# A two-layer decode step in fp32: a ring of 24 KB in place of 28, four KB of K kept across the layers, and one weight tile laid on 20 rows in place of 16

## The chip, the core and the metric

The kernel runs on one core of a Trainium2 chip. The core has a matrix engine (TensorE, in the profile PE for matmuls and PEld for its weight loads), three engines for elementwise work (VectorE or DVE, ScalarE or ACT, GpSimd or POOL), a queue engine that here issues nearly all transfers (SyncE or SP), and sixteen DMA engines that move data between HBM and the on-chip memory of 128 partitions (rows). The metric is the device time of one execution in microseconds.

## The reference

Two layers, each an attention block and a gated feed-forward block, for one new token of four sequences, all in fp32. The same weights and the same caches serve both layers.

```python
B, Sq, D = 4, 1, 512        # Hq, Hkv, Sk, Dh = 32, 8, 4096, 128 ; F = 1792
# A: q = layernorm(x) @ wq ; p = softmax(q k^T / sqrt(Dh)) ; x + (p v) @ wo
# B: h = silu(n @ w1) * (n @ w3), n = layernorm(x) ; x + h @ w2
x = x + _A_ref(_layernorm(x, axis=-1), A_k_cache, A_v_cache, A_wq, A_wo)
x = x + _B_ref(_layernorm(x, axis=-1), B_w1, B_w3, B_w2)
x = x + _A_ref(_layernorm(x, axis=-1), A_k_cache, A_v_cache, A_wq, A_wo)
x = x + _B_ref(_layernorm(x, axis=-1), B_w1, B_w3, B_w2)
```

K and V hold 67 MB each and are needed once in each layer; the weights are 28 MB.

## The kernel before

**Memory.** Nearly all on-chip memory is one tile, `arena` (line 46), of 216 KB on each of 128 partitions. All addresses below are KB in a partition; one KB there is 128 KB of data. Three regions have fixed places: wq at 0 to 64 (WQ), wo at 64 to 128 (WO) and a kept V at 128 to 192 (KEPT). The transposed probabilities pT take the last 2 KB (PT, line 52). What is left in the first feed-forward, 192 to 216 and the first 4 KB of wo's region, is the ring: 28 KB.

**Loads.** `plan` (line 86) is a list of all loads in order: source, KB, keys, and an address or None. `pump` (line 165) issues loads on SP, in this order only, as long as `take` (line 56) finds the place free; `done` (line 196) and `vacate` return a place and call `pump` again. This happens while the program is written out, so the order of SP's instructions and of the places is fixed. On the chip each load then waits only for the instructions that last used its addresses, and for an earlier load's landing, since the loads share eight completion semaphores in turn.

**Layer 0** goes through the eight groups of K and V in order. K of a group is one load of 64 KB a row, and so is V. While K of one group is read, V of the group before is loaded, and so on in turn, in two places (64 and 128). V of the last group (`TURN` = 7) goes to KEPT and stays for layer 1, which takes the groups in the reverse order. wq and wo stay too.

**The ring** (lines 124 to 140). With wq, wo and the kept V in place, the first feed-forward's weights pass through the ring in pieces of one load each: w1 and w3 in two parts ("a" of four 4 KB pieces, "b" of four 3 KB pieces), w2 in seven 4 KB pieces. They are followed by K of the last group for layer 1: its first 32 KB as eight "half" pieces of 4 KB (half of a block of 512 keys), seven of them in the ring. The eighth and all later loads go where `take` finds room, at first in wq's place, whose tiles layer 1's query projection frees one after the other (`q_product`, line 333). TensorE reads the pieces in the order w1a, w3a, w1b, w3b 0 and 1, w2 0, w3b 2 and 3, w2 1 to 6 (`feed_forward`, lines 542 to 587); then come the normalisation and the query projection, and only then the half pieces (`scores`, line 384). The addresses of the pieces, given by `slots`, say which earlier piece a load must wait for: w2 i and half i lie at `slots[i]`; w3b 2 lies where w3a 1 and w3a 3 were; w2 5 waits for w3b 2.

**The tile on few rows.** In the last feed-forward, the first tile of w2 (128 rows of 512) is loaded as 16 rows of 16 KB, `w2s`, by four loads of every fourth row (lines 151 and 154; `pump` takes a slice of rows from line 169 on, line 177 issues it). Each is put ahead of one of w1a, w3a, w1b, w3b. Eight units of 16 rows are then multiplied (`few`, line 536, with `columns`, line 531), four before and four after w3b's product. The hidden values for them come from eight small matmuls (line 562) and one copy (line 567).

## Time and profile before

| | us |
|---|---|
| median of three runs | 706.02 (705.9 to 706.09) |
| the profiled execution | 705.91 |
| its span, first to last instruction | 704.1 |
| mean granted TensorE clock in it | 0.813 of full speed |

The page gives the busy time of each engine in the span, forty slices of the span with the busy share of each engine and of the sixteen DMA engines in tenths, the queues of the DMA engines, and groups of instructions by line. Further views answer for a stretch: busy time and DMA share by window, instructions in order of time with what they waited for, issues of loads with their time to landing. Times in them are from the span's start. In the first layer the groups of K and V last until 337 us; the ring stage is from about 345 to 400; the last feed-forward begins at about 682. A DMA share of 1 means that all sixteen engines have a packet under way; packets on one engine overlap slightly, so it can pass 1. The queue q1 is SP's loads; q8 loads instructions.

### The profile page before, as it was taken

How to read it: one execution, taken by the hardware profiler on the slowest of the kernel's cores; microseconds unless marked ns; L12 is line 12 of the kernel's file. 1: busy time of each engine (PE TensorE's matmuls, PEld its weight loads, DVE VectorE, ACT ScalarE, POOL GpSimd, SP SyncE). 2: the span in 40 equal slices, each digit the busy share in tenths (PEclk: the TensorE clock that was granted, in tenths of full speed). 3: DMA queues.
4: the chain of work that ended last, by engine and by line, in shares of the span. 5: the costliest groups of instructions: out<-in, count | busy, mean ns of one | idle time of the engine just before them, and what ended most of it. 6: DMA issues, size and time to landing. Idle time of an engine off the chain costs nothing. (4 is left out here: it accounts for less than half of the span.)

```text
span 704.1 us, 7082 instructions
## 1 busy us (share of the span) xinstructions
PE 408.4 (58%) x3174; PEld 136.0 (19%) x3174; DVE 85.1 (12%) x291; ACT 36.8 (5%) x85; POOL 2.9 (0%) x10
## 2 busy tenths in 40 slices
PE   2555453456556454547788894364553545477687
PEld 1112011112111111112243231021120111122134
DVE  2001010101001010101111111011000101010111
ACT  0000000000000000002001000000000000000100
POOL 0000000000000000000000000000000000000000
PEclk9986787767777776879999988679787868689899
DMA  9999999999999999999999999999999999999997
GB/s 417 432 403 473 418 417 422 462 418 432 451 421 422 436 448 421 440 408 435 410 405 403 410 437 440 439 436 422 432 455 417 433 432 440 421 433 420 426 425 298
DMA packets 13749, 299.37 MB, mean 425 GB/s; under 512 B 1671, under 2 KB 1799, under 8 KB 6407
## 3 DMA queue, kind: packets, MB, share of 16 engines
q1 hardware_dynamic: 13584, 298.92, 99.2%
q8 instruction: 25, 0.41, 0.2%
q14 instruction: 5, 0.04, 0.0%
q10 hardware_dynamic: 135, 0.01, 0.0%
HBM read 298.85 MB, written 0.07 MB: 425 GB/s over the span
## 5 line engine op out<-in xcount | busy, mean ns | idle before, releaser
L438 PE MATMUL o_ps<-arena 128*32 128x512 f32 x1024 | 148.6, 730 | 147.8 <-DMA arena<-in_v 133.0
L393 PE MATMUL s_ps<-arena,qpad 128*32 128x512 f32 x1024 | 146.2, 725 | 88.0 <-DMA arena<-in_kt 88.0
L438 PEld LDWEIGHTS o_ps<-arena 128*32 128x32 f32 x1024 | 37.7, 130 | 256.8 <-issue 224.5
L393 PEld LDWEIGHTS s_ps<-arena,qpad 128*32 128x32 f32 x1024 | 39.3, 130 | 178.1 <-issue 170.6
L447 DVE SCALAR_TENSOR_TENSOR p<-o_ps,parts,p 128x512 f32<-128x512 f32 x16 | 12.0, 751 | 272.7 <-PE o_ps L438 272.7
L400 DVE TENSOR_REDUCE top<-s_ps 128x1 f32<-128x512 f32 x16 | 11.1, 691 | 190.8 <-PE s_ps L393 190.8
L281 PE MATMUL m_ps<-ident,rows 128*32 128x256 f32 (+2 forms) x90 | 25.2, 376 | 0.0
L445 ACT ACTIVATE p<-o_ps,parts 128x512 f32<-128x512 f32 x16 | 11.0, 687 | 195.8 <-PE o_ps L438 186.9
L337 PE MATMUL o_ps<-arena,xpad 128*32 128x512 f32 x112 | 15.4, 675 | 7.8 <-DMA arena<-in_wq 7.8
L424 PE MATMUL t_ps<-ident,p 128*128 128x128 f32 x64 | 11.4, 305 | 13.5 <-ACT p L418 13.5
L451 PE MATMUL t_ps<-ident,p 128*128 128x128 f32 x64 | 10.5, 287 | 13.9 <-DVE p L447 13.8
L411 ACT ACTIVATE f<-d 128x1 f32<-128x1 f32 x16 | 3.2, 203 | 253.1 <-DVE d L409 253.1
L473 PE MATMUL x_ps<-arena,oT 128*4 128x512 f32 x104 | 12.8, 592 | 6.3 <-DVE oT L459 3.5
L418 ACT ACTIVATE p<-s_ps,top 128x512 f32<-128x512 f32 x16 | 10.9, 684 | 76.7 <-PE t_ps L451 76.7
L425 DVE COPY arena<-t_ps 128x512 f32<-128x512 f32 x16 | 11.1, 691 | 9.7 <-PE t_ps L424 9.7
L451 PEld LDWEIGHTS t_ps<-ident,p 128*128 128x128 f32 x64 | 6.7, 141 | 28.0 <-DVE p L447 28.0
L424 PEld LDWEIGHTS t_ps<-ident,p 128*128 128x128 f32 x64 | 7.3, 150 | 22.3 <-ACT p L418 19.2
L281 PEld LDWEIGHTS m_ps<-ident,rows 128*32 128x32 f32 x90 | 9.4, 110 | 10.4 <-issue 6.3
L506 PE MATMUL o_ps<-arena,xpad 128*32 128x192 f32 (+1 forms) x128 | 8.1, 360 | 1.3 <-DMA arena<-in_w 1.2
L506 PE MATMUL s_ps<-arena,xpad 128*32 128x192 f32 (+1 forms) x128 | 7.9, 359 | 1.6 <-DMA arena<-in_w 1.5
L337 PEld LDWEIGHTS o_ps<-arena,xpad 128*32 128x32 f32 x112 | 3.6, 122 | 17.2 <-DMA arena<-in_wq 8.7
L533 PE MATMUL x_ps<-arena,qT 128*4 128x128 f32 (+1 forms) x168 | 5.9, 271 | 1.1 <-DMA arena<-in_w 1.1
(100 smaller groups left out, 137.3 us busy)
## 6 DMA issues: line engine op xcount, KB each, us to landing
arena<-in_v SPq DMA_DIRECT2D x4, 4096.0 KB, 37.3
arena<-in_w SPq DMA_DIRECT2D x17, 512.0 KB, 9.3
arena<-in_kt SPq DMA_DIRECT2D x8, 1024.0 KB, 10.5
arena<-in_kt SPq DMA_DIRECT2D x2, 4096.0 KB, 16.9
arena<-in_wq SPq DMA_DIRECT2D x1, 7168.0 KB
arena<-in_v SPq DMA_DIRECT2D x3, 2048.0 KB, 36.9
arena<-in_wo SPq DMA_DIRECT2D x1, 4096.0 KB, 24.5
arena<-in_kt SPq DMA_DIRECT2D x8, 512.0 KB, 8.0
```

Of the source, the lines that this page charges most:

```text
L281: nc.tensor.matmul(m_ps[turn["m"] ^ 1][0:32, (4 - w) * P:], rows, ident.unsqueeze(1).broadcast_to([P, w, P]), start=True, stop=True)
L337: nc.tensor.matmul(ps[32 * k:32 * k + 32, :], xpad[:, k, lo:lo + 32], w[:, k, :], start=first, stop=last)
L393: nc.tensor.matmul(s_ps[32 * b:32 * b + 32, :], qpad[:, b, lo:lo + 32], k[:, j, :], start=(blk == 0), stop=(blk == NB - 1))
L400: nc.vector.tensor_reduce(top[:, 0:1], s_ps, axis=AX.X, op=ALU.max, negate=True)
L424: nc.tensor.transpose(t_ps[:, i, :], p[:, i * P:(i + 1) * P], ident)
L425: nc.vector.tensor_copy(pT.rearrange("p i r -> p (i r)"), t_ps.rearrange("p i r -> p (i r)"))
L438: nc.tensor.matmul(o_ps[32 * b:32 * b + 32, :], pT[:, i, 32 * b:32 * b + 32], w[:, b, :], start=(i == 0), stop=(i == NI - 1))
L445: nc.scalar.activation(p, o_ps, AF.Copy, scale=st["parts"][:, 0:1])
L447: nc.vector.scalar_tensor_tensor(p, o_ps, st["parts"][:, 1:2], p, op0=ALU.mult, op1=ALU.add)
L451: nc.tensor.transpose(t_ps[:, j, :], p[:, j * P:(j + 1) * P], ident)
L473: nc.tensor.matmul(x_ps[r:r + B, :], left(2 * i + n), w(n), start=first, stop=False)
L506: nc.tensor.matmul(ps[32 * j:32 * j + 32, lo:lo + n], x32[:, k, :], w[:, j * n:(j + 1) * n], start=(k == 0), stop=(k == KC - 1))
```

## The change

It has three parts.

1. K of the last group in layer 0 is loaded in two parts: 4 KB to a place of its own at 212 (`FIRST`) and 60 KB to 132 to 192. The 4 KB part is the first half piece of layer 1; it is not given back in layer 0 and is not loaded again. pT moves to 210.
2. The ring is 192 to 212 and wo's first 4 KB: 24 KB. The pieces get new addresses. w2 0 is now loaded ahead of w3b 0 and not after w3b 1. What each load waits for follows from the addresses: w2 1 for w1b 3, w2 2 for w3b 0, w2 3 for w3b 1, w2 4 for w2 0, w2 5 for w3b 3, w2 6 for w2 1, half 1 and 2 for w2 2, half 3 to 6 for w2 3 to 6. TensorE's order stays.
3. w2's first tile is laid on 20 rows of 12 KB (six units of 20) and 8 rows of 2 KB (one unit of 8), `w2t`: four loads of five rows and two of four rows. There are seven units, four before and three after w3b's product. The first two loads are put ahead of w1a, the last two ahead of w3b, behind the fourth of `w2s`.

```diff
-FEW = 16
+FEW = 20
...
-    PT = ARENA - 2
-    free = [(WO, PT - WO)]
+    FIRST, PT = ARENA - 4, ARENA - 6
+    free = [(WO, PT - WO), (FIRST, 4)]
...
     def cache(which, layer, g, parts, skip=0):
         src = (kt if which == "k" else v)[g]
+        if (which, layer, g) == ("k", 0, TURN):
+            weights("half", src[:, 0:4 * KB], 0, (4,), 4, FIRST)
+            weights("half", src[:, 4 * KB:], 0, (60,), 4, KEPT + 4, 1)
+            return
...
-    slots = [WO] + [RING + 4 * i for i in (5, 4, 3, 2, 1, 0)]
-    for i in range(4):
-        piece("w1a", i, (slots[6], slots[1], slots[2], slots[3])[i])
-    for i in range(4):
-        piece("w3a", i, (slots[4], slots[5], slots[0], slots[6])[i])
-    for i in range(4):
-        piece("w1b", i, RING + 21 - 3 * i)
-    for i in range(2):
-        piece("w3b", i, RING + 9 - 3 * i)
-    piece("w2", 0, slots[0])
-    for i in range(2, 4):
-        piece("w3b", i, RING + 9 - 3 * i)
-    for i in range(1, 7):
-        piece("w2", i, slots[i])
-    for i in range(7):
-        piece("half", i, slots[i])
+    for name, places in (("w1a", (0, 16, 12, 8)), ("w3a", (4, None, 0, 16)), ("w1b", (13, 10, 7, 4)), ("w2", (None,)),
+                         ("w3b", (1, 16, 13, 10)), ("w2", (6, 2, 16, None, 12, 8)), ("half", (4, 0, 16, None, 12, 8))):
+        first = int(name == "half" or len(places) == 6)
+        for i, at in enumerate(places):
+            piece(name, first + i, WO if at is None else RING + at)
...
-    side = iter([(w2s[i::4], slice(i, FEW, 4)) for i in range(4)])
+    side = iter([(w2s[i::4], slice(i, FEW, 4), 0) for i in range(4)] + [(w2t[i::2], slice(i, 8, 2), 12) for i in range(2)])
...
         for name, w in (("w1", w1), ("w3", w3)):
             aside()
+            if name + part in ("w1a", "w3b"):
+                aside()
...
-                    a = take(n)
+                    a = take(14)
...
-            split = layer == 1 and g == TURN and blk < SPLIT
-            keys = [("half", layer, 2 * blk + i) for i in range(2)] if split else [("k", layer, g, blk)]
+            split = g == TURN and (layer == 0 or blk < SPLIT)
+            keys = [("half", layer if blk or i else 0, 2 * blk + i) for i in range(2)] if split else [("k", layer, g, blk)]
...
             for key in keys:
-                done(*key)
+                if layer or key[2] or not split:
+                    done(*key)
...
-                columns(slice(0, FEW), WT + u, arena[:, at:at + 2 * KB])
+                columns(slice(0, FEW if u < 6 else 8), WT + u, arena[:, at:at + 2 * KB])
...
-            for u in range(8):
-                nc.tensor.matmul(t_ps[0:FEW, 2, B * u:B * u + B], h[0:32, FEW * u:FEW * u + FEW], ident[0:32, 0:B],
+            for u in range(7):
+                n = FEW if u < 6 else 8
+                nc.tensor.matmul(t_ps[0:n, 2, B * u:B * u + B], h[0:32, FEW * u:FEW * u + n], ident[0:32, 0:B],
...
-        few(4, 8)
+        few(4, 7)
...
-        "w2s": lay(w2j[0, :P].reshape(8, FEW, D).transpose(1, 0, 2)).reshape(FEW, 8 * D),
+        "w2s": lay(w2j[0, :6 * FEW].reshape(6, FEW, D).transpose(1, 0, 2)).reshape(FEW, 6 * D),
+        "w2t": lay(w2j[0, 6 * FEW:P]),
```

More of the change, by code (lines that the diff above doesn't have):

```diff
@@ L38, in tile_decode_layers @@
 @with_exitstack
-def tile_decode_layers(ctx: ExitStack, tc: tile.TileContext, x, kt, v, wq, wo, w1, w3, w2, w2s, out):
+def tile_decode_layers(ctx: ExitStack, tc: tile.TileContext, x, kt, v, wq, wo, w1, w3, w2, w2s, w2t, out):
     nc = tc.nc
@@ L148, in tile_decode_layers @@
     cache("v", 1, 0, (32, 16, 16))
-    side = iter([(w2s[i::4], slice(i, FEW, 4)) for i in range(4)])
+    side = iter([(w2s[i::4], slice(i, FEW, 4), 0) for i in range(4)] + [(w2t[i::2], slice(i, 8, 2), 12) for i in range(2)])
     def aside():
-        plan.append((*next(side), "few", None))
+        src, rows, at = next(side)
+        plan.append((src, rows, "few", at))
     for part, per, at in (("a", 4, 0), ("b", 3, 16)):
@@ L175, in pump @@
                     where[keys] = a
-                a = where[keys]
+                a = where[keys] + at
                 nc.sync.dma_start(arena[per, a * KB:(a + n) * KB], src)
@@ L249, in tile_decode_layers @@
     oT = const.tile([P, HKV, REP, B], F32, name="oT")
-    hT = qT.rearrange("p h c -> p (h c)")[:, 0:(WT + 8) * B].rearrange("p (m b) -> p m b", b=B)
+    hT = qT.rearrange("p h c -> p (h c)")[:, 0:(WT + 7) * B].rearrange("p (m b) -> p m b", b=B)
     top = const.tile([P, 32], F32, name="top")
@@ L262, in tile_decode_layers @@
     p = const.tile([P, 512], F32, name="p")
-    pT = arena[:, PT * KB:ARENA * KB].rearrange("p (i r) -> p i r", i=NI)
+    pT = arena[:, PT * KB:FIRST * KB].rearrange("p (i r) -> p i r", i=NI)
     def small(name, n=1, bufs=1):
@@ L566, in feed_forward @@
         if not keep:
-            nc.vector.tensor_copy(hT[0:FEW, WT:WT + 8, :], t_ps[0:FEW, 2, 0:8 * B].rearrange("p (u b) -> p u b", b=B))
+            nc.vector.tensor_copy(hT[0:FEW, WT:WT + 7, :], t_ps[0:FEW, 2, 0:7 * B].rearrange("p (u b) -> p u b", b=B))
             gate(FA, FB)
@@ L624, in tile_decode_layers @@
             if layer and n == 0:
-                assert take(ARENA - PT, PT) == PT
+                assert take(FIRST - PT, PT) == PT
             if n + 1 < HKV:
@@ L632, in tile_decode_layers @@
         if layer == 0:
-            give(PT, ARENA - PT)
+            give(PT, FIRST - PT)
             pump()
```

## The prediction

> **What bounds the kernel now.** I read the page's engine, slice and packet lines first, then the long waits, then the transfers.
>
> ```profile
> PE 408.4 (58%) x3174; PEld 136.0 (19%) x3174; DVE 85.1 (12%) x291; ACT 36.8 (5%) x85; POOL 2.9 (0%) x10
> DMA  9999999999999999999999999999999999999997
> DMA packets 13749, 299.37 MB, mean 425 GB/s; under 512 B 1671, under 2 KB 1799, under 8 KB 6407
> q8 instruction: 25, 0.41, 0.2%
> DVE p L447 <- PE o_ps L438: 272.7, 16, 22.7
> PE o_ps L438 <- DMA arena<-in_v: 133.0, 14, 14.1
> PE s_ps L393 <- DMA arena<-in_kt: 88.0, 16, 12.2
> ```
>
> TensorE is busy 58% of the span and itself waits 133.0 + 88.0 us for V and K; the largest wait, VectorE's 272.7 us, only hangs behind it. The sixteen DMA engines are at 9 tenths or more in 39 of 40 slices. So the bound is bytes over rate, 299.37 MB at 425 GB/s = 704 us. A change is worth what it takes off the DMA engines, as long as none of them is left without queued work. The place to test is the stage with the small ring. The next view is the stage table: length, busy time of PE, PEld, DVE, ACT and POOL, granted clock, DMA share, GB/s.
>
> ```profile
> 345.00:400.00 55.00, 50.19 (x483) 20.37 (x483) 7.32 (x30) 4.08 (x10) 1.10 (x2) 1.00 1.02 404
> 400.00:640.00 240.00, 133.05 (x919) 39.26 (x922) 29.45 (x91) 10.77 (x27) 0.00 (x0) 0.78 1.00 433
> 380.00:382.00 2.00, 1.72 (x20) 0.66 (x20) 0.05 (x1) 0.00 (x0) 0.00 (x0) 1.00 0.96 381
> 388.00:390.00 2.00, 2.00 (x21) 1.14 (x17) 0.17 (x1) 0.00 (x0) 0.00 (x0) 1.00 1.07 385
> ```
>
> The share in the ring's 55 us is 1.02 (packets overlap a little, so just over 1 is full) and its rate is 404 against 433 GB/s: small pieces move more slowly, but nothing stands idle. The two weakest 2-us stretches still have 0.96 and 385 GB/s. The 28 KB ring covers its turn-round; how much is to spare must be worked out.
>
> **The change part by part.** *Four KB of K not loaded again.* The first half block of layer 1 stays from layer 0: one 512 KB transfer less. What such a piece takes shows where TensorE meets each piece as it lands:
>
> ```profile
> 360.07 0.64 PE L506 MATMUL s_ps<-arena,xpad 128*32 128x256 f32 x8 [0.23 <-DMA arena<-in_w]
> ...
> 365.21 0.16 PEld L506 LDWEIGHTS o_ps<-arena,xpad 128*32 128x32 f32 x8 [0.73 <-DMA arena<-in_w]
> ```
>
> Four pieces of 4 KB a row lie between these starts: 5.14 / 4 = **1.28 us** each, which comes off every engine's queue: -1.28. (At the page's mean rate it would be 0.524 MB / 425 GB/s = 1.23.) TensorE's matmuls are the same ones. Layer 0's last K now comes as 4 + 60 KB. The 4 KB piece has its own place and is issued a whole transfer earlier, with nothing waiting behind it on SP; it moves at the piece rate, 1.28 instead of 8.39 MB / 433 GB/s / 16 = 1.21: +0.07.
>
> The Trainium skill, "DMA: Bandwidth & Descriptors", section "Anatomy of one DMA", fits a transfer as about 2.0 us plus its bytes, which speaks against splitting loads and shortening the ring: where no queue covers the fixed part, each such load would pay it (rival 4). The pieces above follow each other at 1.28 us, so before the change a queue covers it.
>
> *Ring of 24 KB.* A slot is filled again only after TensorE has read it. I count, from the two orders in the diff, what is queued behind a piece when its slot's next load waits for it. Before, the least is 19 KB (w2 piece 5 waits for w3b piece 2; 3 + 16 KB lie between). After, it is 13 KB: w2 piece 2 waits for w3b piece 0, with three 3 KB pieces and one of 4 KB between; then 14 KB for w2 piece 3, and 16 KB or more otherwise. In time, by 0.32 us a KB: 6.1 us before, 4.2 us after. Against that stands the turn-round:
>
> ```profile
> 371.18 0.53 PE L506 MATMUL o_ps<-arena,xpad 128*32 128x192 f32 x8 [0.21 <-DMA arena<-in_w]
> 371.77 0.33 SPq L183 DMA_DIRECT2D arena<-in_w  x1
> arena<-in_wq SPq DMA_DIRECT2D x1, 1024.0 KB, 4.8
> ```
>
> 0.59 us from the matmul's start to SP's issue; then the way to the first byte, at most 4.8 - 2 x 1.28 = 2.2 us by the shortest landing of a 1 MB load. Together 2.8. So the slowest DMA engine keeps 4.2 - 2.8 = 1.4 us in hand (before 3.3).
>
> The second narrow place is the layer change, where the ring is full of K and the next space comes from wq:
>
> ```profile
> 382.72 0.33 SPq L183 DMA_DIRECT2D arena<-in_kt  x1
> arena<-in_kt SPq DMA_DIRECT2D x1, 512.0 KB, 8.2
> 385.92 0.33 SPq L183 DMA_DIRECT2D arena<-in_kt  x1
> ```
>
> The last ring load is issued at 382.72 and lands 8.2 us later, at 390.9; the first load into wq's place is issued at 385.92. So 5.0 us are queued on the slowest engine then, 5.0 - 2.2 = 2.8 in hand; with one piece less, **1.5 us**. That engine is not left dry at either place: 0 us on the path. If the cover went, each us beyond it would be added whole.
>
> But engines are not level. Instruction loads (q8) fall on single engines:
>
> ```profile
> q8 instruction: 1, 0.02, 4.5%
> q8 instruction: 12, 0.20, 0.3%
> 697.50:698.00 0.50, 0.50 (x21) 0.49 (x25) 0.00 (x0) 0.00 (x0) 0.00 (x0) 1.00 0.86 344
> ...
> 699.50:700.00 0.50, 0.04 (x4) 0.04 (x8) 0.00 (x0) 0.00 (x0) 0.00 (x0) 1.00 0.62 217
> 700.00:700.50 0.50, 0.50 (x16) 0.29 (x16) 0.00 (x0) 0.00 (x0) 0.00 (x0) 1.00 0.01 4
> ```
>
> The first row is the 1.5 us from 331 on: 4.5% of 16 x 1.5 us, one engine held for 1.1 us; the second is all from 400 on: twelve more. The last rows are the end: engines finish over more than 2 us, and still six tenths of them work at 699.5. An engine that is ahead by more than 1.4 us will run dry in the smaller ring and lose the rest of its lead. That is free unless later instruction loads make that same engine the last. Ends: 0 (only engines that finish early lose lead) and +1.28 (all that is gained is lost by the engine that comes last). There are 12 later loads on 16 engines, so some of those that lose lead do get hit; I take **+0.4**, a third.
>
> *w2's few rows.* Bytes are the same (16 rows x 16 KB = 20 x 12 + 8 x 2 = 256 KB). I assume that each row of such a load is one engine's. By one engine's 425 / 16 = 26.6 GB/s, four engines with 64 KB each (2.46 us) then become four with 52 (2.00) and a fifth with 48 (1.85): -0.46 for the four, +1.85 for the fifth. It counts only on the engine that ends last. The six tenths still at work at 699.5 are ten engines; four of them at most carry these rows, so the last is likely another: 0, ends -0.46 and +1.85. No row of this trace shows on which engines a load of few rows runs. The Trainium skill, "DMA: Bandwidth & Descriptors", section "Why a DMA increments its semaphore by 16 and not by 1", says the lowest-numbered k, with k the largest count up to 16 that divides the rows: 4, 5 and 4 engines here.
>
> The two more small transfers are two more issues on SP, which also waits for earlier landings before issuing:
>
> ```profile
> SPq L177 <- DMA arena<-in_v: 13.8, 2, 9.2
> 685.54 15.05 DMA arena<-in_w
> 691.61 1.05 PE L533 MATMUL x_ps<-arena,qT 16*4 16x128 f32 x32
> ```
>
> The last weights are issued 15 us before they land; even an issue later by the longest of these waits, 9.2 us, leaves 6. One unit of few-row work less takes 8 of these 32 matmuls (four units) off TensorE, 1.05 / 4 = 0.26 us, which lies under the wait for w2's last pieces: 0.
>
> Sum: -1.28 + 0.07 + 0.4 + 0 = **-0.8 us**. The profiled execution took 705.91 us, its span 704.1 and 1.8 around it; that becomes 703.3 + 1.8 = 705.1. The median before is 706.02, 0.11 above the profiled one, so I predict **705.2 us**.
>
> **The rivals.** (1) *The rows of w2 set the end.* Were one of the four engines with 64 KB the last, their 0.46 would come on top and no lead would be given back: 706.02 - 1.21 - 0.46 = 704.35. For it: all the added load is on four engines. Against it: the ten engines at 699.5.
> (2) *The fifth engine becomes last.* If it is among those that finish late, it gets 1.85 us more: 706.02 - 1.21 + 1.85 = 706.6. Against it: six of sixteen engines are done by 699.5, and the fifth may be one of these. The Trainium skill's rule of the lowest-numbered k engines, named above, is what would make it the same engine in all four transfers.
> (3) *All given back.* The engine that ends last loses a whole piece of lead: 706.0. This is also the case of a change that does not do what it says: bytes saved, the slowest queue not shortened.
> (4) *The ring is too short, slower.* Place: w2 pieces 2 and 3, and again the first load into wq's place. Each has 1.4 to 1.5 us in hand on the slowest engine. If the way to the first byte is 3.7 us and not 2.2 (landing takes 8.2 us in this stage, most of it queue), the cover is just gone; at 5.2 us all engines stand 1.5 us at both: -1.21 + 3.0 = +1.8, 707.8. It decides as soon as stalls of the slowest engine pass 1.2 us. Against it: the stage's share of 1.02 shows the present turn-round well covered.
>
> **How the numbers follow.** Forecast, 704.7 to 705.7: 0.62. Rival 1: 0.12. Rival 2: 0.09. Rival 3: 0.11. Rival 4: 0.06. The range 704.3 to 706.6 takes in the forecast, rival 3, and over half of 1 and 2. A measurement of this kernel tells 0.2%, 1.4 us, from no change: faster means under 704.6, slower over 707.4. Rival 1 gives most of its chance to faster, 0.11 in all; rival 4 gives slower 0.05; the rest, 0.84, is the same.
>
> **What would show it.** Packets 299.37 MB less 0.52, and the eighth half block of layer 1 landing about 1.2 us earlier than at 392; between 345 and 400 the share still about 1.0. Fewer GB/s in the 2-us stretches near 372 and 390 would be the leads lost; a share under 0.9 there, with TensorE's waits on in_w grown, is rival 4. At the end, the share in the last 2 us says who is last: a fall to a quarter or less would be rival 1 or 2. A gain of more than 1.7 us, or any loss while the share stays full, would say that a term is missing here.

## The result and the profile after

| | us |
|---|---|
| before, median of ten runs beside it | 706.02 (705.86 to 706.32) |
| after, median of ten runs | 708.01 (706.68 to 709.87) |
| ratio, 95% interval | 1.0026 (1.0018 to 1.0035) |
| the profiled execution after, its span | 708.17, 706.4 |

The changed kernel is slower by 2.0 us, outside the predicted range of 704.3 to 706.6, and its runs scatter over 3.2 us where those before scatter over 0.5. These are the page's engine, slice, packet and queue lines after:

```profile
PE 411.5 (58%) x3164; PEld 136.1 (19%) x3164; DVE 85.1 (12%) x291; ACT 36.8 (5%) x85; POOL 2.9 (0%) x10
DMA  9999999999999999999999999999999999999996
DMA packets 13773, 298.85 MB, mean 423 GB/s; under 512 B 1683, under 2 KB 1811, under 8 KB 6427
q8 instruction: 25, 0.41, 0.2%
```

And the long waits (engine, what it waited for, total, times, longest):

```profile
DVE p L444 <- PE o_ps L435: 276.4, 16, 24.8
...
PE o_ps L435 <- DMA arena<-in_v: 136.6, 15, 15.8
PE s_ps L389 <- DMA arena<-in_kt: 87.1, 17, 12.2
```

The bytes are down by 0.52 MB as meant, and nothing else is new: TensorE still waits for V (136.6 us against 133.0) and K. Only the rate has fallen, from 425 to 423 GB/s, and 298.85 MB at 423 GB/s is 706.5 us. Where it fell, the stage table shows (window, length, busy times, clock, DMA share, GB/s); first after:

```profile
345.00:400.00 55.00, 49.02 (x476) 19.57 (x476) 7.30 (x30) 4.07 (x10) 1.10 (x2) 1.00 1.00 389
356.00:364.00 8.00, 7.17 (x71) 3.62 (x70) 1.65 (x10) 0.95 (x3) 0.55 (x1) 1.00 0.98 383
372.00:380.00 8.00, 6.62 (x84) 2.96 (x83) 0.60 (x2) 0.00 (x0) 0.00 (x0) 1.00 0.98 357
388.00:396.00 8.00, 8.00 (x78) 3.00 (x74) 0.57 (x3) 0.00 (x0) 0.34 (x1) 1.00 1.00 364
400.00:640.00 240.00, 132.02 (x925) 39.75 (x926) 29.47 (x91) 10.76 (x27) 0.00 (x0) 0.80 1.00 433
```

Then before:

```profile
356.00:364.00 8.00, 7.08 (x74) 3.70 (x78) 1.46 (x10) 0.95 (x3) 0.55 (x1) 1.00 1.03 406
372.00:380.00 8.00, 6.01 (x66) 2.43 (x65) 0.55 (x2) 0.00 (x0) 0.00 (x0) 1.00 1.03 403
388.00:396.00 8.00, 8.00 (x78) 3.24 (x78) 0.33 (x2) 0.00 (x0) 0.00 (x0) 1.00 1.01 392
```

The ring's 55 us went from 404 to 389 GB/s, in three places: near 360 (w3a 2 waits for w1a 0), near 375 (w2 2 and 3 wait for w3b 0 and 1), near 390 (the first loads into wq's place). From 400 to 640 the rate is 433 in both. Yet the share in the three places stays at 0.98 to 1.00. No stall of all sixteen engines is seen (at the fewest, 10, 11 and 12 packets are under way in the three places after), only that some engines are short of work.

So engines must be looked at one by one. Each load of 128 rows leaves sixteen completions in the trace; they are taken here as one for each DMA engine. The difference between the last and the first of them is the **lead** of the fastest engine over the slowest; the last is what TensorE waits for. The table gives, for the profiled execution of thirteen of the kernels (the experiments below explain their names), how much later than in the kernel before the last completion of a load comes, and in brackets the lead. Both runs are set equal at wo's last load, just ahead of the ring, and what is not loaded again (1.28 us for 4 KB, 0.64 for 2) is added back, so that 0 means that the slowest engine lost nothing. A profile is one execution, and not always near the median: that of better24 is the fastest of its kernel, those of wait_all, and of ring_only and better24_reload below, are the slowest. "K n" is the load of K or V that lands at about n us in the kernel before, "last" the last load of w2.

```
kernel              w3a 1     w3a 2      w2 2      w2 6    half 7     K 395     K 412     K 432     K 441     K 499     K 520    last
before           0.0(3.3)  0.0(3.3)  0.0(3.3)  0.0(3.2)  0.0(3.0)  0.0(2.5)  0.0(2.2)  0.0(2.2)  0.0(2.2)  0.0(2.2)  0.0(3.6)   0.0(3.8)
change_24        0.0(3.4)  0.0(3.4) -0.2(3.2) -0.2(3.1) -0.2(2.9) -0.1(2.6) -0.2(2.6) -0.2(2.6) -0.1(2.6) -0.2(2.6) -0.3(3.8)  -0.2(4.1)
wait_w3a        -0.1(3.4) -0.1(2.3) -0.2(1.9) -0.2(1.9) -0.1(1.9) -0.1(1.9) -0.1(1.9) -0.2(1.9)  0.2(2.2)  0.2(2.2) -0.1(3.4)   0.1(3.1)
wait_w2          0.0(3.4)  0.0(3.4) -0.2(2.0)  0.0(2.1)  0.1(2.0)  0.1(2.1)  0.1(2.0)  0.1(2.0)  0.1(2.1)  0.1(2.0) -0.2(3.2)   0.1(3.5)
wait_all         0.0(3.2)  0.0(2.3)  1.9(3.8)  1.9(3.2)  2.0(2.4)  2.7(2.9)  3.9(3.4)  3.9(3.4)  4.2(3.7)  4.2(3.7)  2.8(3.7)   4.1(5.1)
better24         0.0(3.3) -0.1(2.3) -0.2(2.1) -0.2(1.8) -0.2(1.6)  0.7(2.3)  0.7(2.2)  0.7(2.2)  0.7(2.1)  0.7(2.1)  0.0(2.8)   1.2(4.0)
keep2           -0.1(3.4) -0.1(2.3) -0.2(2.0)  0.1(2.3)  0.2(2.3)  0.2(2.2)  0.2(2.2)  0.2(2.2)  0.2(2.2)  0.2(2.2)  0.0(3.4)   0.6(4.1)
after           -0.1(3.3) -0.1(2.3) -0.3(1.8)  0.8(1.8)  0.8(1.6)  2.0(2.6)  2.0(2.1)  3.5(3.6)  3.5(3.6)  3.5(3.7)  2.2(3.6)   3.5(4.1)
after_again      0.0(3.5)  0.0(2.4)  0.2(1.7)  2.3(2.9)  2.8(1.4)  4.2(2.6)  4.3(1.9)  5.5(3.2)  5.5(3.2)  5.5(3.2)  4.1(3.2)   5.5(4.6)
before_shift     0.0(3.5)  0.0(3.5) -0.2(3.3) -0.2(3.3) -0.2(2.9) -0.1(2.9) -0.2(2.8) -0.2(2.8) -0.2(2.8)  1.0(4.0)  0.0(4.4)   0.9(4.8)
after_shift      0.0(3.5) -0.1(2.2) -0.2(1.6)  0.1(1.5)  0.2(1.2)  0.2(1.0)  1.4(2.2)  1.4(2.2)  1.5(2.3)  1.5(2.3)  0.1(2.3)   1.5(3.6)
keep2_turn       0.0(3.2) -0.1(2.3) -0.1(2.2)  0.0(2.2)  0.0(2.1)  0.0(2.0)  0.0(2.0)  0.1(2.1)  0.1(2.1)  1.4(3.4)  0.1(3.4)   1.3(4.9)
keep2_turn2     -0.1(3.1) -0.1(2.1) -0.1(2.2) -0.1(2.2)  0.0(2.1)  0.0(2.0)  0.0(2.0)  0.0(2.0)  1.3(3.2)  1.2(3.2) -0.1(3.3)   1.2(4.3)
```

Read the row "after". At w3a 2 the lead falls from 3.3 to 2.3 us, by w2 2 to 1.8, and the slowest engine has lost nothing (-0.3). The loss comes behind it, in steps: by w2 6, at the first K in wq's place, and between K 412 and K 432. At the last step the delay and the lead grow alike (2.0 to 3.5, lead 2.1 to 3.6): some engine was held for 1.5 us while the first one ran on. In the row of before, the lead grows from 2.2 to 3.6 at K 520: that kernel has one such step itself, and the row "after" gets 1.3 back there because its last engine is by then another one.

### The profile page after: what moved, and what is told of

It reads as the page before. It is cut to its first block, busy times and chain, and to the rows that moved or that the text cites. A ratio compares the mean times of both kernels' runs of the same rounds, so it can differ in the third digit from the quotient of the medians.

```text
span 706.4 us, 7064 instructions
## 1 busy us (share of the span) xinstructions
PE 411.5 (58%) x3164; PEld 136.1 (19%) x3164; DVE 85.1 (12%) x291; ACT 36.8 (5%) x85; POOL 2.9 (0%) x10
## 2 busy tenths in 40 slices
DMA packets 13773, 298.85 MB, mean 423 GB/s; under 512 B 1683, under 2 KB 1811, under 8 KB 6427
## 4 chain that ended last, share of the span: by engine, by line
DMA 77%; PE 20%; ACT 1%; issue 1%; SPq 0%; DVE 0%; ACTq 0%
DMA arena<-in_v 56%; PE o_ps L435 16%; DMA arena<-in_w 11%; DMA arena<-in_kt 6%; DMA arena<-in_wo 4%; PE s_ps L389 2%; ACT p L442 1%; PE o_ps L333 1%; PE m_ps L344 0%; PE x_ps L463 0%; PE m_ps L316 0%; PE x_ps L530 0%; SPq L179 0%; PE t_ps L333 0%; PE o_ps L503 0%
## 5 line engine op out<-in xcount | busy, mean ns | idle before, releaser
L435 PE MATMUL o_ps<-arena 128*32 128x512 f32 x1024 | 151.1, 741 | 149.4 <-DMA arena<-in_v 136.6
L389 PE MATMUL s_ps<-arena,qpad 128*32 128x512 f32 x1024 | 148.5, 730 | 87.1 <-DMA arena<-in_kt 87.1
L344 PE MATMUL m_ps<-scaled,p 128*128 128x4 f32 (+1 forms) x32 | 5.1, 293 | 1.9 <-DVE scaled L354 1.4
```

Of the source, the lines that this page charges most:

```text
L389: nc.tensor.matmul(s_ps[32 * b:32 * b + 32, :], qpad[:, b, lo:lo + 32], k[:, j, :], start=(blk == 0), stop=(blk == NB - 1))
L435: nc.tensor.matmul(o_ps[32 * b:32 * b + 32, :], pT[:, i, 32 * b:32 * b + 32], w[:, b, :], start=(i == 0), stop=(i == NI - 1))
```

## The experiments

The reference time of before was 706.11 us in the first group, 706.12, 706.10, 706.05 and 706.01 in the later ones.

**The parts alone.** w2_only makes part 3 in the kernel before; ring_only makes parts 1 and 2 without part 3 (the diff of the change, cut there). ring28_less keeps the ring of 28 KB and does not load half block 0; it leaves out the first half block of K (the second is read in its place), so it has the bytes of the change without its cost in room:

```diff
-    for i in range(7):
-        piece("half", i, slots[i])
+    for i in range(1, 8):
+        piece("half", i, slots[i % 7])
...
-            keys = [("half", layer, 2 * blk + i) for i in range(2)] if split else [("k", layer, g, blk)]
+            keys = [("half", layer, max(2 * blk + i, 1)) for i in range(2)] if split else [("k", layer, g, blk)]
```

ring24_reload is the changed kernel that loads half 0 again, into the same 4 KB, behind w2 6: the bytes of before, a ring of 24 KB for the weights, 28 KB of K queued when the layers change.

```diff
+        if name == "half":
+            piece("half", 0, FIRST)
...
-            keys = [("half", layer if blk or i else 0, 2 * blk + i) for i in range(2)] if split else [("k", layer, g, blk)]
+            keys = [("half", layer, 2 * blk + i) for i in range(2)] if split else [("k", layer, g, blk)]
```

> The kernel before with the third part alone: w2's first tile on 20 and 8 rows, six small loads; ring 28 KB, K loaded as before. Theory A (the short ring lets the DMA engines run dry): between 705.5 and 706.1 us, as before, or up to 0.46 us less. Theory B (the new rows and their two more loads cost the time): about 708.0 us, the whole loss.

> The changed kernel with the third part undone: ring of 24 KB and 4 KB of K kept, w2's first tile on 16 rows in four loads. Theory A: the loss stays, 707.5 to 708.5 us, scattered over some 2 us from run to run as with the whole change. Theory B: the saving of one piece shows, 704.8 us.

> The kernel before with the ring of 28 KB and the first half block of K not loaded in layer 1 (the second is read in its place); the eighth half block goes into the ring slot that this leaves. 512 KB less, ring as long as before. Theory A: the saving shows, -1.2 to -1.3 us, 704.8 us, with little scatter. If the engine that ends last is not helped by fewer bytes (the all-given-back rival), 706.0 us.

> The changed kernel, but the first half block of K is loaded again in layer 1, into the place where it was kept: the bytes of before, 24 KB of ring for the weights, 28 KB of K queued at the change of layer. If the loss is mostly made at the change of layer (queue of 24 KB in place of 28 KB there): about 706.0 to 706.5 us, better than the whole change in spite of 1.28 us more to load. If it is made among the weights: 708.5 to 709.3 us, the whole change plus 1.28.

| kernel | median, lowest to highest | ratio to before, 95% |
|---|---|---|
| w2_only | 705.99, 705.78 to 706.95 | 0.9999 (0.9989 to 1.0009) |
| ring_only | 708.83, 706.49 to 710.3 | 1.0030 (1.0014 to 1.0047) |
| ring28_less | 704.77, 704.57 to 705.04 | 0.9980 (0.9971 to 0.9989) |
| ring24_reload | 707.65, 707.03 to 709.85 | 1.0026 (1.0017 to 1.0036) |

w2's rows make no difference that can be seen (the interval reaches from 0.8 us less to 0.6 more). Theory A held for w2_only and ring28_less; ring_only, at 708.83, lies above its 708.5, and B (704.8) fell there. The piece is worth 706.11 - 704.77 = 1.34 us where the ring keeps its length. So the shorter ring costs 1.99 + 1.34 = **3.3 us** in the changed kernel; 1.5 of it (707.65 - 706.11) is there with all bytes loaded and 28 KB of K queued when the layers change. Neither expectation for ring24_reload met that (706.0 to 706.5 and 708.5 to 709.3). In its trace the last engine has lost only 0.1 us by w2 6 and 1.3 by K 432, so a short ring for the weights is enough for this part, but it doesn't fall due among the weights. The stage rows of ring28_less and of ring24_reload:

```profile
345.00:400.00 55.00, 50.20 (x487) 20.36 (x487) 7.30 (x30) 4.08 (x10) 1.10 (x2) 1.00 1.02 406
```

```profile
345.00:400.00 55.00, 48.96 (x477) 19.67 (x477) 7.32 (x30) 4.08 (x10) 1.10 (x2) 1.00 1.01 396
356.00:364.00 8.00, 7.38 (x80) 3.73 (x71) 1.82 (x10) 0.95 (x3) 0.55 (x1) 1.00 0.98 373
372.00:380.00 8.00, 6.77 (x83) 3.17 (x85) 0.42 (x1) 0.24 (x2) 0.00 (x0) 1.00 1.01 365
388.00:396.00 8.00, 8.00 (x76) 3.01 (x70) 0.58 (x3) 0.00 (x0) 0.21 (x1) 1.00 1.03 416
```

With 28 KB the stage runs at 406 GB/s. With 24 KB for the weights and 28 KB of K, the two early places are as weak as after (373 and 365 GB/s) and the third is whole again (416).

**Each place alone, in the kernel before.** wait_w3a makes w3a 2 wait for w1a 0; wait_w2 leaves 14 KB queued behind the piece that w2 2 waits for; change_24 puts half 6 into wq's place, so that 24 KB are queued when the layers change; wait_both is the first with the third, wait_all all three. All load the bytes of before. The edits, in this order:

```diff
-        piece("w3a", i, (slots[4], slots[5], slots[0], slots[6])[i])
+        piece("w3a", i, (slots[4], slots[5], slots[6], slots[0])[i])
...
+    slots[2], slots[4] = slots[4], slots[2]
     for i in range(1, 7):
         piece("w2", i, slots[i])
...
-    for i in range(7):
+    for i in range(6):
         piece("half", i, slots[i])
...
+    piece("half", 6, None)
     piece("half", 7, None)
```

> The kernel before, with 28 KB of ring and all of its bytes; only two places are exchanged, so that w3a piece 2 goes where w1a piece 0 was and waits for TensorE to read it, as it does after the change, and w3a piece 3 goes into wo's place. Theory A (engines that run dry are the loss, and the first place where they do is this wait): 3 to 7 engine-us idle between 356 and 364, and 706.3 to 706.9 us. Theory C (the loss comes only at the tight pieces of w2 and at the layer change): 706.0, within 0.2 of before, whether or not engines fall idle at 356 to 364.

> The kernel before, with all of its bytes and its ring of 28 KB for the weights; half block 6 of K goes into wq's place instead of the ring, so that 24 KB and not 28 KB are queued when the layers change. Theory A: engines run dry at 388 to 396 (some 10 engine-us idle) and nowhere else, and the time is 1.0 to 1.7 us above before, 707.0 to 707.7: the whole change less the loss among the weights that the run with half 0 loaded again showed. Theory C2 (the layer change costs nothing by itself, it only adds because leads were already lost among the weights): 706.0 to 706.4.

> The kernel before with all its bytes and two of the edits tried alone put together: w3a piece 2 waits for w1a piece 0, and 24 KB of K instead of 28 are queued when the layers change. Theory E (a queue that runs dry costs little by itself, since only the leads of engines that are ahead are used up; the next short queue then finds no leads and stops the late engines as well): more than the sum of the two, 707.0 to 707.7 us, and more than 3 engine-us idle at 388 to 396. Theory F (each place has its own price, and the prices add): 0.3 + 0.0 above before, 706.2 to 706.5.

> The kernel before with all its bytes; the places of w2 pieces 2 and 4 (and of half blocks 2 and 4) are exchanged, so that w2 piece 2 has 14 KB queued behind the piece that it waits for, as after the change, and every other load as much as before. Theory E: leads are used up at 372 to 380 (3 to 7 engine-us idle) and 706.0 to 706.5 us. Theory F: the place carries what the run with half 0 loaded again lost beyond the wait of w3a piece 2, 1.5 - 0.3, so 706.9 to 707.5.

> The kernel before with all its bytes and all three waits together: w3a piece 2 behind w1a piece 0, w2 piece 2 with 14 KB queued, 24 KB of K at the layer change. Theory E: nearly what the short ring cost in the changed kernel (3.3 us), 708.0 to 709.3. Theory F: the sum of the three alone.

| kernel | median, lowest to highest | ratio to before, 95% |
|---|---|---|
| wait_w3a | 706.37, 705.86 to 709.7 | 1.0009 (1.0000 to 1.0018) |
| change_24 | 706.04, 705.82 to 706.57 | 1.0000 (0.9992 to 1.0009) |
| wait_both | 706.22, 706.04 to 706.45 | 1.0001 (0.9993 to 1.0010) |
| wait_w2 | 706.27, 706.05 to 706.71 | 1.0003 (0.9995 to 1.0012) |
| wait_all | 707.39, 706.14 to 709.86 | 1.0021 (1.0011 to 1.0031) |

By the medians, one place costs 0 to 0.25 us, two of them 0.1, all three 1.3; the intervals of the single places reach up to 0.6, 0.8 and 1.3 us, and the twelve times of wait_all run from 706.14 to 709.86. wait_w3a doesn't decide between theories A and C. Theory A had 1.0 to 1.7 us for the layer change alone: it fell there, and C2 (nothing by itself) held. Theory E had 0.9 us or more for wait_both: it fell there, and wait_all stayed below its 708.0 to 709.3. It held for wait_w2 (706.0 to 706.5). Theory F fell at wait_w2 (0.9 us or more expected), and at wait_all, which costs nearly four times the sum of the parts (0.25 - 0.08 + 0.17 = 0.3). The place of w3a 2 shows in wait_w3a's row as it does after:

```profile
356.00:364.00 8.00, 7.13 (x75) 3.71 (x78) 1.50 (x10) 0.95 (x3) 0.55 (x1) 1.00 0.98 382
```

The rate falls from 406 to 382 GB/s and 1.1 us of lead goes (3.4 to 2.3), but the slowest engine is not delayed, and nearly nothing is lost at the end. wait_w2 ends the same way, with a lead of 2.0. What the places take away is the lead; whether that costs anything is decided later.

**Other places for the pieces, and half of the change.** better24 has the changed kernel's 24 KB with other addresses: w2 0 behind w3b 1 again, 16 KB or more queued behind each piece that a load waits for, 18 at w2 3. better24_reload loads half 0 again in it, as ring24_reload does. keep2 keeps only a quarter block, 2 KB, with a ring of 26 KB and at least 18 KB queued.

```diff
-    for name, places in (("w1a", (0, 16, 12, 8)), ("w3a", (4, None, 0, 16)), ("w1b", (13, 10, 7, 4)), ("w2", (None,)),
-                         ("w3b", (1, 16, 13, 10)), ("w2", (6, 2, 16, None, 12, 8)), ("half", (4, 0, 16, None, 12, 8))):
+    for name, first, places in (("w1a", 0, (0, 16, 12, 8)), ("w3a", 0, (4, None, 0, 16)), ("w1b", 0, (13, 10, 4, 7)),
+                                ("w3b", 0, (None, 0)), ("w2", 0, (16,)), ("w3b", 2, (10, 13)),
+                                ("w2", 1, (4, None, 0, 16, 8, 12)), ("half", 1, (4, None, 0, 16, 8, 12))):
```

The edit of keep2 to this:

```diff
-    FIRST, PT = ARENA - 4, ARENA - 6
+    FIRST, PT = ARENA - 2, ARENA - 4
...
+            weights("q", src[:, 0:2 * KB], 0, (2,), 2, FIRST)
+            weights("q", src[:, 2 * KB:], 0, (62,), 2, KEPT + 2, 1)
...
+    for name, first, places in (("w1a", 0, (0, 16, 12, 8)), ("w3a", 0, (4, None, 0, 18)), ("w1b", 0, (15, 12, 8, 4)),
+                                ("w3b", 0, (None, 0)), ("w2", 0, (18,)), ("w3b", 2, (15, 12)),
+                                ("w2", 1, (8, 4, None, 0, 18, 12)), ("q", 1, (16,)), ("half", 1, (8, 4, None, 0, 18, 12))):
...
+                keys = [("q", 0, 0), ("q", 1, 1), ("half", 1, 1)]
```

> The changed kernel, with other places and one other order for the same pieces in the same 24 KB: w2 piece 0 comes behind w3b piece 1 again, and at least 16 KB are queued behind the piece that a load waits for, 20 KB for w2 piece 2 at 17 KB and piece 3 at 18 KB in place of 13 and 14. Theory A: nothing idle at 372 to 380, the idle times at 356 to 364 and 388 to 396 stay; 0.5 to 1.0 us less than the changed kernel, 707.0 to 707.5. If most of the loss among the weights comes from those two pieces: 706.5. Theory D (a ring of 24 KB costs what it costs wherever the pieces lie): 708.0.

> Half of the change: 2 KB of K kept in place of 4 (one quarter block), a ring of 26 KB, the 2 KB beside it loaded alone, w2's rows as changed. 0.26 MB are saved, half of 1.28 us, 0.64. At least 18 KB are queued behind each piece that a load waits for; w3a piece 2 still waits for w1a piece 0. Theory A (cost rises from nothing once the queue is shorter than the way round): idle at 356 to 364 as after, under half as much as after at 388 to 396; 705.6 to 706.4. Theory D (cost in proportion to the ring's loss, 3.3 us for 4 KB): 706.02 - 0.64 + 1.65 = 707.0.

> The ring of 24 KB with the other places (at least 16 KB queued, 18 for w2 piece 3), and half 0 loaded again into its own place, so the bytes of before and 28 KB of K at the layer change. Only the wait of w3a piece 2 and waits of 16 to 18 KB are left of the change. Theory E: 706.2 to 706.7, as with the wait of w3a piece 2 alone, and the 1.8 us that the same places cost without the reload come from the layer change. Theory F: 706.62 + 1.28 = 707.9, since 24 KB of K at the layer change cost nothing by themselves.

> The version with 2 KB kept and a ring of 26 KB once more, timed again to see whether it is faster than before at all: 705.5 us if the first timing holds (0.6 below before); 706.1 if that was chance.

| kernel | median, lowest to highest | ratio to before, 95% |
|---|---|---|
| better24 | 706.62, 705.73 to 708.37 | 1.0009 (1.0000 to 1.0017) |
| better24_reload | 707.40, 705.97 to 708.12 | 1.0017 (1.0008 to 1.0025) |
| keep2 | 705.52, 705.21 to 706.72 | 0.9994 (0.9986 to 1.0003) |
| keep2_again | 705.61, 705.16 to 706.51 | 0.9994 (0.9986 to 1.0003) |

Other addresses in the same 24 KB take 1.4 us off the changed kernel, more than theory A's 707.0 to 707.5 and close to the 706.5 that was expected if w2 2 and 3 made most of the loss among the weights; theory D (24 KB cost what they cost) fell. The rows of better24 at the first two places:

```profile
356.00:364.00 8.00, 7.13 (x75) 3.68 (x78) 1.52 (x10) 0.95 (x3) 0.56 (x1) 1.00 1.00 383
372.00:380.00 8.00, 5.97 (x70) 2.51 (x73) 0.60 (x2) 0.00 (x0) 0.00 (x0) 1.00 1.02 398
```

The place near 375 is mended (398 GB/s against 357 after); the one near 360 stays (383), since there every address of the 24 KB waits for w1a 0 or a later piece. better24 still costs 706.62 - 706.12 + 1.34 = 1.8 us of ring. better24_reload missed both expectations (706.2 to 706.7 by E, 707.9 by F), so that its 1.3 us was foreseen by no theory that goes by places alone. For keep2, theory D (707.0) fell as well. keep2 comes out 0.4 to 0.6 us below before, twice; each interval still takes in 1, so a gain is likely and not shown. Its rows at the second and third place are whole:

```profile
372.00:380.00 8.00, 6.05 (x66) 2.43 (x65) 0.53 (x2) 0.00 (x0) 0.00 (x0) 1.00 1.03 410
388.00:396.00 8.00, 8.00 (x78) 3.13 (x74) 0.41 (x3) 0.00 (x0) 0.00 (x0) 1.00 1.02 411
```

**One engine at a time.** The steps in the first table were taken up by the next runs. after_again is the changed kernel once more. before_shift and after_shift add 64 idle matmuls to layer 0, where TensorE waits for V; keep2_turn does the same to keep2, and keep2_turn2 adds 128 (without the condition on f):

```diff
+                if layer == 0 and 1 <= g <= 4 and f and i == 0:
+                    for _ in range(16):
+                        busy(1)
```

> The changed kernel once more, for a second profile. Theory H: the first engine's lead over the last falls from 3.3 to about 2.3 us at w3a piece 2 and below 2 at w2 piece 2, as in the first profile, with no delay of the last engine up to there; behind it steps of 0.5 to 1.5 us, at places that differ from the first profile's, since it is chance which engine an instruction load or a slow packet meets. Theory G: the same steps at the same places, within 0.2 us.

> The kernel before with 64 more idle matmuls early in layer 0 (their results are not used), 128 instructions of TensorE, half of what one instruction load brings: the instruction loads later on come half a step earlier (near 357, 373, 387, 403 and 424 us in place of 366, 379, 394, 413 and 435). Theory H (a delay of one DMA engine, by an instruction load of 1.0 to 1.1 us or by slow first packets after an empty queue, adds to the time only where that engine's lead over the slowest one is used up): leads of 2 to 3 us cover the loads wherever they fall, 705.8 to 706.4, highest minus lowest under 1 us. Theory G (the loads play no part): the same.

> The changed kernel with the same 64 idle matmuls early in layer 0. Theory H: the step by which the slowest engine falls back near 413 us (1.5 us in the profile of the changed kernel) is not there; a step of up to 1.1 us stands instead at one of the moved loads (373, 387, 403, 424) or none; 707.0 to 708.5, scattered over more than 2 us. Theory G: the same steps at the same places as in the changed kernel, one at 413 to 417 among them, and 708.0.

> The version with 2 KB kept and a ring of 26 KB, with 64 more idle matmuls early in layer 0 (their results are not used). In the kernel before they brought one instruction load more, at no later place but one, and each later load then came one turn later in the order of the DMA engines. Theory H: the time moves by about one load, 1.0 to 1.3 us, up or down, by whether a load now falls on the engine that ends last or not: 704.4 to 704.8 or 706.4 to 706.9; 705.5 only where the last engine is hit as often as without them. Theory G (loads play no part, only the idle matmuls' time on TensorE, which waits for data there): 705.5.

> The same with 128 idle matmuls, so two instruction loads more and every later load two turns on. Theory H: again 1.0 to 1.3 us up or down, or none, by which engine is hit, and not the same as with one turn. Theory G: 705.5, as with one turn.

| kernel | median, lowest to highest | ratio to before, 95% |
|---|---|---|
| after_again | 710.29, one run | |
| before_shift | 707.38, 707.11 to 707.98 | 1.0019 (1.0010 to 1.0028) |
| after_shift | 706.75, 705.79 to 708.6 | 1.0014 (1.0005 to 1.0024) |
| keep2_turn | 706.61, 706.36 to 707.5 | 1.0009 (1.0000 to 1.0018) |
| keep2_turn2 | 706.80, 706.38 to 708.18 | 1.0011 (1.0002 to 1.0020) |

after_again has the same fall of the lead as after (3.5 to 2.4 to 1.7) and steps behind it at the same places: by w2 6 the last engine falls back 2.1 us in place of 1.1, by K 395 another 1.4 in place of 1.2, and by K 432 1.2 in place of 1.5. So the lead falls alike in both, and the first step differs by 1.0 us: theory H was right on the fall and on sizes that change, theory G on the places but not on the sizes.

The idle matmuls did something else than was written of before_shift and after_shift: the instruction loads did not move in time. before_shift missed both expectations (705.8 to 706.4). after_shift missed theory H's range by 0.25 us at its lower end, but has no step at K 432, as H had it; G fell. The 64 idle matmuls are 128 TensorE matmuls and 128 weight loads on before_shift's page, and they bring one whole instruction load (page lines):

```profile
PE 421.8 (60%) x3302; PEld 152.7 (22%) x3302; DVE 85.1 (12%) x291; ACT 36.8 (5%) x85; POOL 2.9 (0%) x10
...
q8 instruction: 26, 0.43, 0.2%
```

256 instructions and one 16 KB load more agree with the Trainium skill, "Runtime: NRT & Kernel Launch", section "Instruction fetch mechanics", which gives blocks of 16 KiB or 256 instructions. The same section calls the cost of crossing such a block mostly hidden; here, as it seems, it is hidden only as long as the DMA engine that carries the block is not the last one. The loads behind the ring come at the times of before, but each has one more ahead of it, and the time goes up by 1.3 us in the kernel before. In the changed one the median is 1.3 lower, but the intervals of after and after_shift overlap (1.0018 to 1.0035 and 1.0005 to 1.0024). Where before_shift loses, its row in the table says: by K 499 (1.0 us, lead 2.8 to 4.0) and again at the very end. Each has an instruction load just ahead of it. These are the queue rows of before from 510 to 513 and of before_shift from 483 to 486 and from 696 to 698 (loads, MB, share of sixteen engines); keep2_turn from 483 to 486 and keep2_turn2 from 435 to 438 have the same 2.3%:

```profile
q8 instruction: 1, 0.02, 2.3%
```

```profile
q8 instruction: 1, 0.02, 2.2%
...
q8 instruction: 1, 0.02, 3.4%
```

2.3% of 16 x 3 us is 1.1 us on one engine. Counted from the start of the program, with the times of the instruction loads in the trace, and in brackets the time from a last completion ahead of the step to one behind it, beside the same interval where there is no step:

```
kernel        loads   load, at      step of the last engine        eight loads later, at   step
before        25      17th, 510.8   1.4 (20.74 us, 19.35 usual)    25th, 700.0             none
before_shift  26      17th, 484.1   1.1 by K 499                   25th, 696.4             1.1 (3.61 us, 2.49 usual)
keep2_turn    26      17th, 483.6   1.3 by K 499                   25th, 695.6             1.2 (3.73 us, 2.49 usual)
keep2_turn2   27      17th, 435.5   1.2 by K 441                   25th, 688.7             1.3 (4.94 us, 3.69 usual)
after         25      14th, 413.1   1.5 by K 432                   22nd, 675.1             1.5 (11.34 us, 9.79 usual)
after_again   25      14th, 415.2   1.2 by K 432                   22nd, 677.9             1.4 (6.31 us, 4.89 usual)
after_shift   26      14th, 394.3   1.2 by K 412                   22nd, 644.4             1.4 (11.14 us, 9.72 usual)
```

Theory H had put keep2_turn at 704.4 to 704.8 or 706.4 to 706.9; G, with 705.5, fell. That two turns would give another time than one did not come out (706.80 and 706.61), another place of the step did. Each load put in ahead moves the step one load forward, from 511 to 484 to 435, and the next step comes eight loads later, as long as the last engine still has work then. In the changed kernel, with its leads cut, the steps stand behind the 14th and the 22nd load instead, in all three traces, as if another engine had become the last. This fits instruction loads that go to eight DMA engines in turn.

The same turn makes the leads, ahead of the ring. In the kernel before, the lead grows from 0.4 to 1.7 us behind the 1st load (46.0) and from 1.9 to 3.3 behind the 9th (331.4), and each of the twenty traces has this second growth behind its 9th load, wherever that one falls (260.6 in keep2_turn2). From 400 us on, every step of over 0.5 us in the twenty traces has load 13, 14, 17, 21, 22 or 25 ahead of it (once 23), and none has 15, 16, 18, 19 or 20. The trace doesn't name the engine of a load, so the turn is argued. That steps of 1.1 to 1.5 us follow certain loads, which take 1.0 to 1.1 us, and move when loads are put in ahead, is shown; what makes some steps longer than the load is not.

The scatter of the changed kernel has another source. By K 395 the last completion is 0.2 us late in after_shift, 2.0 in after and 4.2 in after_again, and these executions took 706.12, 708.17 and 710.29 us: they part in the ring stage, and behind it all three have the same two steps.

## Why the prediction was wrong

**TensorE is not the bound, the bytes are:** right. Sixteen engines at 9 tenths in 39 of 40 slices after as before, and the bytes fell as counted.

**-1.28 for the half block:** right, 1.34 with the ring left alone (ring28_less). The 0.07 for loading 4 + 60 KB was not tried by itself.

**w2's rows, 0:** right, 705.99 against 706.11 in w2_only. Rival 2 (+1.85) is out. Rival 1's -0.46 is inside the interval; the median, 0.12 lower, speaks against it. The loads leave 5, 5, 5, 5, 4 and 4 completions in the trace in place of four times 4, which fits one engine for each row, as the prediction assumed.

**"So the slowest DMA engine keeps 1.4 us in hand":** right for the waits among the weights. Up to w2 2 the slowest engine is delayed by no more than 0.2 us in both profiles of the changed kernel. The Trainium skill, "DMA: Bandwidth & Descriptors", section "Anatomy of one DMA — SWDGE (gpsimd) path", would put some 2 us of fixed time on each load that no queue covers; its fit is of loads issued from GpSimd, and these are SP's. At the waits of w3a 2 and w2 2 none of it reaches the last engine (-0.1 and -0.3). At the layer change, where the prediction also had 0 us on the path, it was not so. The time in hand came out as counted: half 7 was issued at 386.85 and the last ring load landed at 390.59, 3.7 us later, which less the 2.2 leaves 1.5. Yet the last completion fell back by 1.2 us at K 395 (1.4 in after_again, 0.9 in better24, 0.1 in change_24). The two stretches that the prediction calls the weakest are misread: the lowest rates in that view are 379 GB/s from 390 to 392 and 381 from 380 to 382. Nothing rests on it.

**"An engine that is ahead by more than 1.4 us will run dry in the smaller ring and lose the rest of its lead":** right, and seen: 3.3 us become 1.8.

**"I take +0.4, a third. Ends: 0 and +1.28":** this is the step that failed. It is the prediction's only term for what the shorter ring costs, by lost leads, and its size was wrong by a factor of eight: 3.3 us by the medians. That the leads go was right; three things were missing. First, the upper end. I had let the last engine lose at most what the change gains, but nothing ties the two: without leads a later hold-up of one engine can make a new last engine, and the table has steps of 1.1 + 1.2 + 1.5 us in the profiled execution. Second, the chance of being hit. I had spread 12 later loads over 16 engines; in the traces every eighth load strikes again, so an engine that is last when its turn comes pays at each turn. Third, the hold-ups before 400, 2.3 us of the loss in that profile (1.1 + 1.2). Instruction loads cost 1.1 us each, as counted, but there are also slow packets. In the trace's packet records, the two 8 KB packets that took longest at 391 after took 1.5 and 1.7 us; the median of 828 such packets from 395 to 440 is 0.31. Summed over the packets of 388 to 400 that take over 0.15 us more than usual for their size, the excess is about 6 us of one engine before, 3 in after_shift, 13 in after, 21 in after_again and 25 in ring_only, and the step at K 395 is 0.0 in after_shift, 1.2, 1.4 and 2.9 in the last three. From 372 to 380 the excess is some 10 us after, against 2 before; but ring24_reload has 13 there and loses only 0.1 us by w2 6. So slow packets go with the step at the layer change; that they cause it is not shown.

**"16 KB or more otherwise":** the count was right and the conclusion not. w3a 2 has 20 KB queued behind w1a 0, but w1a 0 has landed (356.4) 1.5 us before TensorE begins to read it (357.9): the output projection and the normalisation come first. There engines run dry first (383 GB/s after, 382 in wait_w3a with 28 KB of ring).

**"Rival 4, 707.8":** right in size (708.01) and place, given a chance of 0.06, and not in its mechanism. It had all engines standing 1.5 us at two places. The share there is 0.98 to 1.00, each place alone costs 0 to 0.25 us, and only together do they cost more than the sum. In after_again, which at 710.29 us is over each of the ten times of after, and in ring_only's profile (710.3) the third place does come to a stop of most engines (at the fewest, one and two packets are under way), the row that rival 4 had asked for; the rows of 388 to 396 in these two:

```profile
388.00:396.00 8.00, 8.00 (x68) 3.15 (x71) 1.58 (x9) 0.37 (x1) 0.55 (x1) 1.00 0.78 262
```

```profile
388.00:396.00 8.00, 8.00 (x52) 2.99 (x56) 1.34 (x7) 0.37 (x1) 0.55 (x1) 0.74 0.88 284
```

In after_again the last engine was already 2.8 us late at half 7. As it seems, the stop is a consequence: late weights make the query projection late, and so wq's place; no run separates that. Part of it can be TensorE itself, a rival that no run tests. In the ring stage its granted clock falls to 0.5 in four of the twenty traces: for 6.8 us from 385.3 in ring_only (the 0.74 above), and for 3.4 us from 383.3 in after_again, 379.1 in wait_all and 385.6 in better24_reload, four executions of 708.1 to 710.3 us. Just ahead of it in after_again, TensorE had waited 1.9 us for w2 5. A slower TensorE gives wq's places back later. In the profile of after (708.17) the clock is 1.00 throughout that stage, so the loss of that execution doesn't come from there.

**The range** missed for the same reason: its upper bound came from the cap of +1.28.

What stays open: which slow packet or instruction load made each step before 400, and why packets are slow at the narrow places. No run here separates the two. better24_reload's 1.3 us and the sum in wait_all are explained by lost leads only in the sense that their leads were short (2.3 us at w3a 2) and steps followed. Leads of 1.9 to 2.0 us at w2 2 stand in wait_w3a, wait_w2 and keep2 too, and little followed there (0.1, 0.1 and 0.6 us by the last load): a short lead doesn't cost by itself.

## What to carry to other kernels

Where transfers bound a kernel, a queue of transfers has two uses: it keeps the slowest DMA engine busy, and it lets the others get ahead. A buffer cut down until only the first still holds looks full in the views by shares, and then a later hold-up of one engine can go to the end; look at first and last completion of a load, not at the mean share. And test such a cut with some instructions more or less: in the kernel before, 256 of them moved the time by 1.3 us, so a gain of that size can be a matter of which engine is hit.

## What the runs showed of the hardware that was not expected

- An instruction load of 16 KB holds one DMA engine for 1.0 to 1.1 us, and 256 TensorE instructions more in a stage where TensorE only waits made the kernel before 1.3 us slower (1.0019, 1.0010 to 1.0028) and keep2 1.0 to 1.1 by the medians (705.52 and 705.61 to 706.61; the intervals just overlap).
- The kernel before has such a step of its own: its 64 KB loads of K and V end at 460.6, 480.0, 499.3, 520.1 and 539.4, each 19.3 to 19.4 us after the one ahead, but 20.7 at 520.1, just behind the load at 510.8.
- A wait that leaves several engines idle for a moment (at the fewest, nine packets were under way between 356 and 360 in better24) delayed the last engine by nothing (-0.1), while the steps at K 441 and K 499 leave the share of that stretch at 1.
